# A linear-attention and PReLU network kernel: the first four steps in a new order, and GpSimd's fills ahead of its masks

## The chip, the cores and the metric

The kernel runs on one core of a Trainium2 chip. A core has five engines with queues of their own: TensorE (PE in the profile, its weight loads PEld), VectorE (DVE), ScalarE (ACT), GpSimd (POOL) and SyncE (SP, which here only issues DMAs). The metric is the time of one execution on the device in microseconds (us), as the median of several runs.

## The reference

Two blocks, one behind the other. For each of 4 batches and 8 heads, with 768 tokens of 48 dimensions, a gated linear attention:

```python
f = 1.0 / (1.0 + np.exp(-f_logit))
for t in range(S):
    state = f[:, :, t, :, None] * state + np.einsum('bhd,bhe->bhde', k[:, :, t], v[:, :, t])
    y[:, :, t] = np.einsum('bhd,bhde->bhe', q[:, :, t], state)
```

Its output, laid out as 3072 tokens of 384, goes through a network with 2048 hidden units:

```python
h = x @ w_in
g = np.maximum(h, 0.0) + alpha * np.minimum(h, 0.0)
return g @ w_out
```

All of it in float32.

## The kernel before

The work is cut into 12 **steps**: a step is one pair of batches (`bp`, 0 or 1) and one chunk `c` of 128 tokens (0 to 5), so steps 0 and 1 are the first chunk of both pairs, steps 2 and 3 the second, and so on. Within a chunk the recurrence is written as products: f is multiplied up over ranges of 4, 32 and 64 tokens, scores of q and k are formed within those ranges, masked into a matrix `A`, and `A` and the carried state multiply v.

Each stage of a step is a Python generator; every `yield` ends a piece. The order in which all pieces are emitted is written out by hand in the string `START` (up to step 4; `USUAL` repeats a pattern from step 5 on). That order is the queue order of TensorE, VectorE, ScalarE and SyncE. Each of these takes its instructions strictly in it and waits at the first one whose inputs or buffers aren't ready. GpSimd's order is not written out: a planner makes it from the order in which the instructions are emitted and from what it takes to be ready.

The letters of the string, with the number of the step behind them; P1.3 below means the third piece of P in step 1:

- **P** prepares. P.1 loads f, q, k, v (on SP for step 0, on GpSimd's queue for steps 1 to 4). P.2 on ScalarE: sigmoid of f (L298), copies of f and q (L299, L301). P.3 on VectorE: products of f (`kr`, `fs`) and q times f (`qd`; L310 to L320). In the first chunk (steps 0 and 1): P.4 has ScalarE's copies into the tile `us` (L341, L343), k times its products (L354), L355 and the first small products (L378, L383, L385); P.5 has L387, which writes `k16` inside `us`, L390 and L378; P.6 two scans (L347, L348) and the keys `kh`, `ks` (L414, L419); P.7 the queries `q3` (L408, L447); P.8 ScalarE's copies of them into `A` (L454).
- **S** and **T** are the scores of the two halves u = 0 and 1 of a step: .1 TensorE k times `qd` (L580, PSUM `pair0` or `pair1`), .2 VectorE's masked copies into `ad` (L589), .3 TensorE k4 times `us` (L580), .4 masked copies again (L615 in the first chunk, L599 later).
- **O** carries the state. In the first chunk: .1 TensorE `k16` times `q16` (L490), .2 ScalarE's copies into `ad` (L495), .3 VectorE L503 and TensorE `kh` times `q3` (L512), .4 ScalarE's copies into `A` (L519), .5 eight transposes of `ks` on TensorE (L529), .6 ScalarE's copies to `ksn` (L533), .7 TensorE `ksn` times v (L543), .8 ScalarE's copies into the state (L559). Step 0 uses the PSUM tiles `more0` and `more1`, the others `pair0` and `pair1`.
- **Y** attends: .1 and .2 ScalarE's copies of `ad` into `A` (L623), .3 TensorE `A` times v (L634), .4 ScalarE's copy y (L641), VectorE's update of the state (L553, twice L557) and, for all steps but the first, ten DMAs that turn y into xT (L664). Step 0 turns it on TensorE in Y0.5 instead (xt, L653, copied by L655).
- **n** is the network: eight pieces of ph (L679: twelve matmuls of 128x256), ScalarE's neg (L684) and VectorE's gate (L686), then the product with w_out (po, L699, for step 0; pa to pe, L718, later).
- **a** and **w** bring w_in in eight pieces of 256 columns: a issues the load on SP into one of three buffers (L234) and has ScalarE take it apart (L238, L239), w has VectorE put it together (L248). **b** and **g** do the same for w_out. The first load writes into a buffer that P0.2 touches last, so that it goes out behind q. In step 0, the k-th ph needs the k-th piece of w_in. **W** (L784) forms sums of w_out's quarters.
- **X** gives the PSUM tiles `more0` and `more1` back; the network's four banks and xt's come out of them.
- **i** multiplies ones by ones (L790, 128x256) and **j** does 16 tiny matmuls (L798). Both write `more0`, and nothing reads it.
- **K**, **M** (from step 2 on) move the keys by DMA.

The constants are filled and the masks are made on GpSimd before the first step: `mraw` (for L589), `mquad` (for L599), `mhalf` (for L615), `ident` and `dense` (for Y0.5), and two fills inside `us` for each of steps 0 and 1, `k16[16:32]` to zero (L335) and `g16[3:5]` to one (L336), which stand in P.4.

Of the kernel before, what the change touches and what calls it, by code (L numbers as in the profile page):

```python
# [8 lines left out]
F32 = mybir.dt.float32  # L9
I16 = mybir.dt.int16  # L10
# [8 lines left out]
DB = 32  # L19
MASKED = (1, 0)  # L20

U = 2
CH = 64
NC2 = C // CH
NB = DB // 4
WP = 768
RAWS, LEADS = 3, 4
# [1 line left out]

BEGUN = 5  # L30
START = (
    "i P0:4 j T0 P0:2 S0 P0 a O0:2 T0 P1 P0 O0 T0 S0 O0 P1 S0 a O0 P1 T0 S0 P1 O0:2 Y0 i P1 Y0 O0 S1 w Y0 "
    "a Y0 X a w O1 Y0 w O1 w S1 P1 a n0 w a:2 P1 n0 a T1 P1 P2 b S1 T1 S1 n0 w:2 n0 T1 O1 P2 T1 b P2 n0 w "
    "O1 g n0 b O1 P2 g:2 b Y1 g b P2 n0:2 O1 n0 O1 b:3 g:2 O1 g n0 Y1:2 g W:2 P2 n0 Y1 T2 W S2 P2 P3 T2 "
    "S2 P3 n0 n1 P3 T2 S2:2 T2 n1:3 P2 K2 Y2 W O2 T3 n1 Y2 T3 n1 M2 W O2 n1:2 O2 P3 n1 P3 O2 P3 n1 Y2:2 "
    "n1 P3 n1 S3 K3 n1 S3 n2 T3:2 P4 S3 n2:2 S3 n2 P4 n2:2 M3 P4 n2:3 P3 O3:3 Y3 O3 P4 Y3 n2 P4 Y3 n2 Y3 "
    "P4 S4 T4 S4 n2 T4 P5 n2 P4 n3:2 K4 P5 n3 S4 T4:2 n3 S4 n3:2 M4 P4 P5 n3:2 Y4 O4:2 Y4 O4 n3 P5 n3 O4 "
    "Y4:2 P5 n3:2 P5:3 K5 n3 "
)
USUAL = "T:2 S:2 n:4 M T:2 S n P+ S n P+ n:3 Y O P+ O:2 Y O n P+ Y:2 P+ n:3 P+:3 K+"  # L40

LOOSE = ("a", "w", "b", "g", "W", "i", "j", "X")

def flat(start, usual, steps=12):
    out = []
    for word in start.split():
        key, _, times = word.partition(":")
        out += [(key,) if key in LOOSE else (key[0], int(key[1:]))] * int(times or 1)
    for n in range(BEGUN, steps + 1):
# [11 lines left out]
def kernel(  # L61
# [30 lines left out]
    nc = tc.nc  # L92
    B, NC, _, HP, _ = qT.shape
    DM = v.shape[-1]
    H = 2 * HP
# [5 lines left out]
    W = U * HP * C  # L101
    GC = W // CH
    G = W // DB
    NJ = C // DB
    NQ = 4
    UO = [0, 0]
    for m in range(1, NB):
        UO.append(UO[-1] + (DB if m == 1 else DB - 4 * m))
    UW = UO.pop()
    VO = [0, 0, DB, DB + 16]  # L110
    VW = DB + 24
# [6 lines left out]
    work = ctx.enter_context(tc.tile_pool(name="work", bufs=2))  # L118
    staging = ExitStack()
    stage = staging.enter_context(tc.tile_pool(name="stage", bufs=1))  # L120
# [41 lines left out]

    mraw = const.tile([128, 4, NB, 4], F32, tag="mraw", name="mraw")
    nc.gpsimd.memset(mraw, 0.0)
    diag = lvl[:, 1].rearrange("p (i r) -> p i r", r=4)
    for d in range(4):
        nc.gpsimd.tensor_copy(mraw[:, d, :, d:4], diag[:, :, 0:4 - d])
    inq = const.tile([128, NB], F32, tag="inq", name="inq")
    nc.vector.tensor_reduce(inq, diag, mybir.AxisListType.X, ALU.add)
    mquad = const.tile([128, UW], F32, tag="mquad", name="mquad")  # L170
    nc.gpsimd.memset(mquad, 0.0)
    for m in range(1, NB):
        lo = UO[m] + (4 if m == 1 else 0)
        n = NB - m
        nc.gpsimd.tensor_copy(mquad[:, lo:lo + 4 * n].rearrange("p (i r) -> p i r", r=4),
                              inq[:, 0:n].unsqueeze(2).broadcast_to((128, n, 4)))
    mhalf = const.tile([128, VW], F32, tag="mhalf", name="mhalf")
    nc.gpsimd.memset(mhalf, 0.0)
    for half in range(2):
        for m in range(1, NQ):  # L180
            n = NQ - m
            lo = 16 * half + 4 if m == 1 else VO[m] + 4 * n * half
# [4 lines left out]


    A = const.tile([128, U, H, C], F32, tag="A", name="A")
    nc.gpsimd.memset(A, 0.0)  # L190
    ident = const.tile([128, 128], F32, tag="ident", name="ident")
    make_identity(nc, ident)
    nc.gpsimd.tensor_scalar(om, om, -1.0, 1.0, ALU.mult, ALU.add)
# [3 lines left out]
    nc.gpsimd.memset(dense, 0.0)  # L197
    for par in range(2):
        nc.gpsimd.tensor_copy(dense[:, (2 + par) * D:(3 + par) * D], ident[:, 64 * par:64 * par + D])

    first = {"raw": stage.tile([128, WP, 4], I16, tag="raw", name="w_in_raw0", bufs=RAWS)}

    def load_weights(dst, src, name):

# [60 lines left out]
    def quads(t):  # L265
        return t.rearrange("p (n r) -> p n r", r=4)

    def halves(cc):

        return slice(CH * cc, CH * cc + CH), slice(CH * (1 - cc), CH * (1 - cc) + D)  # L270

    def prepare(bp, c, x):

        i = f"{bp}_{c}"
        b0 = U * bp
        ahead = steps.index((bp, c))
        loads = nc.gpsimd if 0 < ahead < 5 else nc.sync

        def load(name, src, bufs=2):
            t = work.tile([128, W], F32, tag=name, name=f"{name}_{i}", bufs=bufs)  # L280
            tu = t.rearrange("p (u x) -> p u x", u=U)
            parts = [slice(u, u + 1) for u in range(U)] if name == "f" and not ahead else [slice(0, U)]
            for p in parts:
                loads.dma_start(out=tu[:, p], in_=src[b0:b0 + U, c].rearrange("u p h t -> p u (h t)")[:, p])
            return t

        f = quads(load("f", fT, 1))
# [3 lines left out]
        for cc in range(NC2):  # L291
            t_, _ = halves(cc)
            loads.dma_start(out=vs[bp][t_, cc, :, 0:DM], in_=v[b0:b0 + U, c, t_].rearrange("u t d -> t u d"))
        yield

        by_u = [slice(u * G * NB // U, (u + 1) * G * NB // U) for u in range(U)] if not ahead else [slice(0, G * NB)]
# [28 lines left out]


        ps = work.tile([128, NS], F32, tag="ps", name=f"ps_{i}", bufs=1)
        ut = work.tile([128, G * UW], F32, tag="us", name=f"us_{i}", bufs=1)
        if c:
            us = ut.rearrange("p (g t) -> p g t", g=G)  # L330
        else:

            at = (0, VW, VW + 16, VW + 16 + DB, VW + 16 + DB + NB)
            us, q16, k16, g16 = (ut[:, G * lo:G * hi].rearrange("p (g t) -> p g t", g=G) for lo, hi in zip(at, at[1:]))
            nc.gpsimd.memset(k16[:, :, 16:DB], 0.0)  # L335
            nc.gpsimd.memset(g16[:, :, 3:5], 1.0)  # L336
            x["q16"], x["k16"] = q16, k16
        x["us"] = us
        q4 = us[:, :, 0:DB].rearrange("p g (i r) -> p g i r", r=4)
# [136 lines left out]
    def carry(bp, c, x):  # L476

        i = f"{bp}_{c}"
        home = more if (bp, c) == steps[0] else pairs
        off = home[0]  # L480
        if not c:
            half = home[1]
            for u in range(U):
                for hp in range(HP):
                    for j in range(NJ):
                        g = (u * HP + hp) * NJ + j
# [8 lines left out]
                nc.scalar.copy(ad[:, u, :, :, 16:DB], half[:, :, o:o + HP * 16].rearrange("p r (h t) -> p r h t", h=HP))  # L495
            yield
        q3, ks, kh, pre = (x[n] for n in ("q3", "ks", "kh", "pre"))
        f64 = work.tile([128, U, H], F32, tag="f64", name=f"f64_{i}")
        by64 = pre.rearrange("p (a c j) i -> p a c j i", c=NC2, j=2)
        for cc in range(0 if c else 1, NC2 if c < NC - 1 else 1):  # L500
            for par in range(2):
# [3 lines left out]
        for u in range(U):  # L505
            for hp in range(HP):
                a = (u * HP + hp) * NC2
# [15 lines left out]
        if not c:  # L523
            yield
            pk = home[1]
            for u in range(U):
                for hp in range(HP):
                    a = (u * HP + hp) * NC2
# [281 lines left out]
    with tc.manual_schedule(engines={mybir.EngineType.PE, mybir.EngineType.DVE, mybir.EngineType.Activation,  # L810
                                     mybir.EngineType.SP}):
        run = {}
        for n, step in enumerate(steps):
            x = {}
            for key, stage_ in zip("POYKMn", (prepare, carry, attend, keys_moved, landed, network)):
                run[key, n] = stage_(*step, x)
            run["S", n], run["T", n] = (scores(u, *step, x) for u in range(U))
        for key in ORDER:
            next(run[key] if key in run else pieces[key[0]])
# [55 lines left out]
```

## Time and profile before

| | before |
|---|---|
| median of 3 runs | 602.92 us (602.43 to 603.97) |
| profiled execution | 602.81 us, span 601.0 us |
| busy: TensorE, VectorE, ScalarE, GpSimd | 575.6, 494.7, 247.4, 85.4 us |
| mean granted clock of TensorE | 0.999 |
| DMA | 50.36 MB |

The span is the time from the first to the last instruction; 1.8 us of the execution lie around it. A row of the profile names the source line, engine, operation and tiles, the number of instructions, and what ended the engine's idle time before them; the chain of waits follows the work that ended last back from the end. On TensorE a float32 matmul of the program stands as two matmuls. A few records of matmuls can be missing.

### The profile page before, as it was taken

The page shows a single profiled execution, that of the slowest core. Times are in us where ns is not written, and L with a number is a line of the kernel's source. Part 1 is how long each engine was busy: PE and PEld are TensorE (multiplying, and loading weights), DVE is VectorE, ACT ScalarE, POOL GpSimd, SP SyncE. Part 2 cuts the span into 40 slices and gives each one's busy share as a digit, 9 for nine tenths or more (in the row PEclk, how much of TensorE's full clock was granted, in tenths as well). Part 3 has the DMA queues.
Part 4 walks back from the last instruction along what each step waited for, and adds up shares of the span by engine and source line. Part 5 has one row for each costly group of instructions (what it writes and reads, how often), then busy time and mean ns, then how long its engine had stood idle before and what let it go on. Part 6 is the DMA issues. An engine that isn't in the chain of part 4 may idle for free.

```text
span 601.0 us, 18092 instructions
## 1 busy us (share of the span) xinstructions
PE 575.6 (96%) x7760; PEld 516.8 (86%) x7760; DVE 494.7 (82%) x998; ACT 247.4 (41%) x430; POOL 85.4 (14%) x162
## 2 busy tenths in 40 slices
PE   2489999999999999999999999999999999999997
PEld 1378667898899899899899899899899899899997
DVE  7989998997888779988988988988988987882351
ACT  5679952621461450550461451452343344232110
POOL 9210014013002103001200300300300300300000
PEclk9999999999999999999999999999999999999999
DMA  8778736015005302502601601601601511201000
GB/s 263 254 216 295 249 89 125 1 48 130 2 2 161 52 1 59 156 1 56 157 2 55 159 3 56 158 2 41 170 4 30 155 31 27 55 1 29 27 1 27
DMA packets 52880, 50.36 MB, mean 84 GB/s; under 512 B 26720, under 2 KB 43360, under 8 KB 52800
## 3 DMA queue, kind: packets, MB, share of 16 engines
q1 hardware_dynamic: 42784, 37.46, 21.7%
q0 software_dynamic: 5504, 9.90, 6.7%
q10 hardware_dynamic: 4512, 1.85, 1.3%
q8 instruction: 61, 1.00, 0.7%
q14 instruction: 19, 0.16, 0.1%
HBM read 36.21 MB, written 4.72 MB: 68 GB/s over the span
## 4 chain that ended last, share of the span: by engine, by line
PE 88%; DVE 7%; ACT 2%; POOL 1%; issue 1%; DMA 0%; DVEq 0%; ACTq 0%; POOLq 0%
PE ph L679 40%; PE pa L718 10%; PE pc L718 10%; PE pair L580 6%; PE pe L718 5%; PE pd L718 5%; PE pb L718 5%; PE pair L634 3%; PE pair L543 1%; DVE w_out_sb L248 1%; PE pair L512 1%; PE po L699 1%; DVE gate L686 1%; POOL mhalf L183 1%; DMA f<-in_fT 0%
## 5 line engine op out<-in xcount | busy, mean ns | idle before, releaser
L679 PE MATMUL ph<-xT,w_in_sb 128*128 128x256 f32 x1152 | 255.3, 381 | 1.4 <-DVE w_in_sb L248 1.4
L679 PEld LDWEIGHTS ph<-xT,w_in_sb 128*128 128x128 f32 x1152 | 216.9, 190 | 33.4 <-issue 2.4
L686 DVE SCALAR_TENSOR_TENSOR gate<-neg,om,ph 128x256 f32<-128x256 f32 x192 | 81.2, 476 | 33.0 <-ACT neg L684 33.0
L684 ACT ACTIVATE neg<-ph 128x512 f32<-128x512 f32 x96 | 56.1, 594 | 121.2 <-PE ph L679 101.6
L718 PE MATMUL pa<-w_out_sb,gate 128*128 128x192 f32 x352 | 62.1, 330 | 0.0
L718 PE MATMUL pc<-t,S 128*128 128x192 f32 x352 | 61.6, 328 | 0.0
L454 ACT COPY A<-q 48x512 f32<-48x512 f32 x44 | 27.1, 617 | 83.4 <-DVE q L408 82.9
L718 PEld LDWEIGHTS pa<-w_out_sb,gate 128*128 128x128 f32 x352 | 57.4, 190 | 1.3
L464 POOL DMA_DIRECT2D ksn<-kt x80 | 46.2, 586 | 85.9 <-DVE kt L422 61.3
L718 PEld LDWEIGHTS pc<-t,S 128*128 128x128 f32 x352 | 57.4, 190 | 0.4
L664 POOL DMA_DIRECT2D xT<-y x22 | 11.9, 544 | 287.5 <-ACT y L641 287.4
L599 DVE COPY_PREDICATED ad<-mquad,pair 128x224 f32<-128x224 int32 (+6 forms) x140 | 41.7, 299 | 4.1
L589 DVE COPY_PREDICATED ad<-mraw,pair 128x256 f32<-128x256 int32 (+1 forms) x96 | 41.2, 451 | 4.0 <-PE pair L580 0.8
L364 DVE TENSOR_TENSOR us<-us,fs 128x768 f32<-128x768 f32 (+5 forms) x60 | 36.9, 615 | 1.1
L765 DVE TENSOR_TENSOR S<-gate 128x512 f32<-128x512 f32 x44 | 30.3, 688 | 0.8
L718 PE MATMUL pe<-w_out_sb,S 128*128 128x192 f32 x176 | 30.6, 327 | 0.0
L718 PE MATMUL pb<-t,gate 128*128 128x192 f32 x176 | 30.4, 326 | 0.0
L718 PE MATMUL pd<-w_out_sb,S 128*128 128x192 f32 x176 | 30.4, 326 | 0.0
L623 ACT COPY A<-ad 32x512 f32<-32x512 f32 x48 | 29.4, 613 | 0.6
L641 ACT COPY y<-pair 128x512 f32<-128x512 f32 x22 | 11.8, 589 | 43.4 <-PE pair L634 43.4
L718 PEld LDWEIGHTS pe<-w_out_sb,S 128*128 128x128 f32 x176 | 28.8, 190 | 0.2
L718 PEld LDWEIGHTS pb<-t,gate 128*128 128x128 f32 x176 | 28.9, 190 | 0.0
(125 smaller groups left out, 710.6 us busy)
## 6 DMA issues: line engine op xcount, KB each, us to landing
w_out_raw<-in_w_out SPq DMA_DIRECT2D x8, 767.8 KB, 7.9
w_in_raw<-in_w_in SPq DMA_DIRECT2D x8, 767.2 KB, 9.5
out<-o SPq DMA_DIRECT2D x23, 192.0 KB, 1.9
q<-in_qT SPq DMA_DIRECT2D x8, 512.0 KB, 4.6
k<-in_kT SPq DMA_DIRECT2D x8, 512.0 KB, 7.1
f<-in_fT SPq DMA_DIRECT2D x7, 512.0 KB, 3.9
vs<-in_v SPq DMA_DIRECT2D x16, 192.0 KB
ksn<-kt SPq DMA_DIRECT2D x80, 32.0 KB, 2.2
```

What stands on the lines that cost most here:

```text
L364: nc.vector.tensor_tensor(us[:, :, UO[m]:UO[m] + 4 * n].rearrange("p g (i r) -> p g i r", r=4), us[:, :, skip:skip + 4 * n].rearrange("p g ...
L454: nc.scalar.copy(A[halves(cc)[1], :, par * HP:(par + 1) * HP, CH * cc:CH * (cc + 1)], q3[rows(par)].rearrange("p (u h c) s t -> p u h c (s ...
L464: (nc.gpsimd if a % 2 else nc.sync).dma_start(out=ksn[32 * b:32 * (b + 1)].rearrange("p u (h x) -> p (u h) x", h=HP)[:, :, 32 * a:32 * a + n],
L580: nc.tensor.matmul(to[DB * j:DB * (j + 1), par, hp * step + lo:hp * step + hi], lhsT=keys[r_, g * DB:(g + 1) * DB], rhs=by[r_, g, lo:hi], ...
L589: nc.vector.copy_predicated(adu[:, :, :, d:4], mraw[:, d, :, d:4].bitcast(I32).unsqueeze(1).broadcast_to((128, H, NB, n)), rv[:, :, QO[d]: ...
L599: nc.vector.copy_predicated(ad[:, u, :, :, 4 * m:DB], mquad[:, lo:lo + n].bitcast(I32).unsqueeze(1).unsqueeze(1).broadcast_to((128, 2, HP, ...
L623: nc.scalar.copy(A[s_].rearrange("p u h t -> p (u h) t")[:, :, s_], ad[s_].rearrange("p u r h t -> p (u r h) t"))
L679: nc.tensor.matmul(ph[:, j * T:(j + 1) * T], lhsT=w_in_sb[:, kt, m * 128:(m + 1) * 128], rhs=xT[:, kt], start=(kt == 0 and j == 0), stop=( ...
L684: nc.scalar.activation(neg, phv, AF.Relu, scale=-1.0)
L686: nc.vector.scalar_tensor_tensor(gate[:, m % NH, m // NH], neg[:, j], om[:, m:m + 1], phv[:, j], ALU.mult, ALU.add)
L718: nc.tensor.matmul(to[:, 0:DH], lhsT=of(f), rhs=by(f), start=(f == 0 and not more), stop=(f == NH - 1), skip_group_check=True)
L765: nc.vector.tensor_tensor(to, x_, y_, op)
```

## The change

Three things change.

- `START` is a new order of the same pieces. Both `i` are gone, the one `j` moves behind S0.4, and from the pieces around step 5 on the order is as it was. In the new order step 0's P0.5 follows P0.4 directly; S goes ahead of T in step 0; step 1's P1.2 stands ahead of O0.4; the first piece a1 stands behind O0.4 and P1.3 in place of ahead of O0.1; P1.4 and P1.5 stand together ahead of Y0.1, O0.5, S1.1 and O0.6; O1.1 stands behind Y0.5 in place of ahead of it; w7 and w8 stand behind n0.4; Y1.3 stands behind n0.11.
- Step 0's fills of `us` (L335, L336) are emitted directly behind `mraw`'s fill and ahead of all masks, by a function `of_halves`. The fill of `A` moves behind `dense`.
- `mquad` is filled in a function that is called behind step 1's loads (P1.1).

`f64` is also kept in the step's dictionary, and `LOOSE` has one more letter; neither adds an instruction.

```diff
 START = (
-    "i P0:4 j T0 P0:2 S0 P0 a O0:2 T0 P1 P0 O0 T0 S0 O0 P1 S0 a O0 P1 T0 S0 P1 O0:2 Y0 i P1 Y0 O0 S1 w Y0 "
-    "a Y0 X a w O1 Y0 w O1 w S1 P1 a n0 w a:2 P1 n0 a T1 P1 P2 b S1 T1 S1 n0 w:2 n0 T1 O1 P2 T1 b P2 n0 w "
-    "O1 g n0 b O1 P2 g:2 b Y1 g b P2 n0:2 O1 n0 O1 b:3 g:2 O1 g n0 Y1:2 g W:2 P2 n0 Y1 T2 W S2 P2 P3 T2 "
...
+    "P0:3 S0 P0:2 T0 O0 P0:2 O0 P1 S0 O0 P1 S0 O0 T0 S0 j P1 a T0 P0 T0 P1:2 w Y0 O0 S1 O0 Y0 O0:2 a Y0:2 "
+    "a P1 w P1 X Y0 w O1 a w a:2 n0 O1 S1 w a n0 w a n0:2 w:2 b O1 T1:2 O1 n0 b g n0 g b S1 T1:2 b P2 n0 "
+    "P2 S1 b P2 g n0 g P1 n0 O1 b O1 b g:2 Y1 n0 O1 g b Y1 O1 S2 P2 n0 g S2 P2 W P2 Y1:2 P2 n0 T2 O2 P3 "
...
     nc.gpsimd.memset(mraw, 0.0)
+    at = (0, VW, VW + 16, VW + 16 + DB, VW + 16 + DB + NB)
+
+    def of_halves(ut):
+
+        parts = [ut[:, G * lo:G * hi].rearrange("p (g t) -> p g t", g=G) for lo, hi in zip(at, at[1:])]
+        nc.gpsimd.memset(parts[2][:, :, 16:DB], 0.0)
+        nc.gpsimd.memset(parts[3][:, :, 3:5], 1.0)
+        return parts
+
+    first = {"us": work.tile([128, G * UW], F32, tag="us", name="us_first", bufs=1)}
+    first["parts"] = of_halves(first["us"])
...
     mquad = const.tile([128, UW], F32, tag="mquad", name="mquad")
-    nc.gpsimd.memset(mquad, 0.0)
-    for m in range(1, NB):
-        lo = UO[m] + (4 if m == 1 else 0)
...
-    nc.gpsimd.memset(A, 0.0)
...
+    nc.gpsimd.memset(A, 0.0)
...
+    def quads_of_mask():
+
+        nc.gpsimd.memset(mquad, 0.0)
+        for m in range(1, NB):
...
+        if ahead == 1:
+            quads_of_mask()
         yield
...
-            nc.gpsimd.memset(k16[:, :, 16:DB], 0.0)
-            nc.gpsimd.memset(g16[:, :, 3:5], 1.0)
+            us, q16, k16, g16 = of_halves(ut) if ahead else first["parts"]
```

## The prediction

> **What bounds the kernel now.** Read first: busy shares by slice (15 us each), on the page.
>
> ```profile
> PE   2489999999999999999999999999999999999997
> DVE  7989998997888779988988988988988987882351
> ```
>
> From the third slice on TensorE is full, to the end. Its matmuls are the same before and after (bar two warming pairs), so the span is the time at which the full stretch begins, plus that work, plus holes in it. The second view, what TensorE waited for, gives the holes:
>
> ```profile
> PE pair L580 <- ACT us L341: 5.7, 1, 5.7
> PE more L543 <- ACT ksn L533: 3.5, 1, 3.5
> PE more L490 <- DVE us L390: 3.4, 1, 3.4
> PE more L512 <- DVE q L408: 2.3, 1, 2.3
> PE ph L679 <- DVE w_in_sb L248: 1.4, 1, 1.4
> PE more L490 <- issue: 0.6, 1, 0.6
> ```
>
> All but the 1.4 fall before 40 us (the timeline puts that one at 64.92 to 66.28; after 42.55 there is only one more, 0.25 at 87.87). Third, the chain of waits in order of time, which tells who is late in the first 40 us:
>
> ```profile
> 6.27 2.35 POOL mquad L175 x5
> 8.62 3.44 POOL mhalf L183 x6
> ...
> 13.46 0.22 POOL us L336
> ...
> 13.70 0.69 DVE us L387
> ...
> 23.18 1.07 ACT f L298
> ...
> 29.65 1.08 ACT ksn L533 x2
> ...
> 32.31 1.15 PE more L790 x2
> 33.46 1.27 PE pair L580 x64
> 34.73 2.81 PE more L634 x60
> ...
> 39.89 2.83 PE xt L653 x12
> ```
>
> GpSimd's masks hold VectorE, VectorE and ScalarE hold TensorE; 32.31 is the second warming pair `i`. Last, TensorE's timeline, for its pace:
>
> ```profile
> 25.36 1.97 PE L529 MATMUL more<-ident,ks 128*128 128x128 f32 x8
> 37.56 1.58 PE L490 MATMUL pair<-us 48*32 48x16 f32 x128
> 61.29 1.04 PE L529 MATMUL pair<-ident,ks 128*128 128x128 f32 x8
> ```
>
> The same eight transposes take 1.97 us at 25 and 1.04 at 61: 214 and 109 ns apart. TensorE begins at half pace. In step 0's L634 the timeline has 34 matmuls from 34.66 to 36.53 (55 ns each) and 30 from there to 37.56 (34 ns); the trace's record of the granted clock sets in at 36.65 (the page's PEclk, full from the start, tells nothing of the time ahead of it). The full clock came 5.87 us into the one long unbroken run of the start, which begins at 30.78 with L543. Nothing shorter brought it (25.36 to 27.33, for one).
>
> **The change part by part.** Pieces are named by step and place: P1.3 is the third piece of P of step 1.
>
> *GpSimd's fills.* VectorE waited 1.49 us at L387 (12.21 to 13.70) for the fill L336. That fill now precedes the masks, so the wait goes whole. Moving mquad's seven copies (3.05 us) behind step 1's loads lets those issue sooner: GpSimd reached them at 13.55, so 10.5 now, but f's old contents are read until 11.4 (L355), so about 11.5. mquad itself is first read at 102.74 (L599): 90 us of cover, cost nothing. If that cover were gone, 3.05.
>
> *VectorE.* From L387 at 12.21: P0.5 to P0.7 take 6.65 (13.70 to 20.35), giving 18.86; S0.2 1.60, the two L503 0.49, T0.2 1.60: 22.55; S0.4 (half of L615's 1.82) 23.46; P1.3 3.64: 27.10; T0.4 0.91: 28.0. Before, both halves were done at 29.73, so 1.7 earlier: the 1.49 and 0.2 that P1.3 waited for the sigmoid. No wait of VectorE's lies in between if step 1's f is ready by 23.5.
>
> *ScalarE.* The first weight piece a1 (L238, L239: 1.6) moves from 12.2 to behind O0.4, P1.2 moves ahead of O0.4. From P1.2 to the end of P1.4 it has 2.7 + 1.5 + 1.6 + 1.25 (L454) + 2.4 = 9.4 us of work and must be through by 28.0, so P1.2 must start by 18.6. f lands 3.9 us (its row's median) to 5.4 (k's) after an issue at 11.5, at 15.4 to 16.9, so it holds. Behind P1.2 wait O0.4, then `j` on TensorE (it writes the PSUM that O0.4 reads), then T0.3; T0.3's result isn't wanted before 27.1, so 3 us of slack.
> Then Y0.1 1.25 (28.05 to 29.3), O0.6 1.08 (30.4), L543 1.53 (32.0), L559 0.96 (33.0), and L634 starts at 33.1 where it started at 34.66. The removed second `i` (1.15) lay on that path, but L543 could not start before L533, so its removal is within these 1.5 us and not added again. The first `i` lay in a 5.66 us wait for others: nothing.
>
> *L634 to the network.* At half pace throughout, 64 x 55 ns = 3.5: to 36.6 (before 37.56). To xt it was 2.35 (L553, both L557): xt at 38.95, against 39.89. But O1.1 (L490, 1.41 busy) ran in that wait before and now stands behind xt: 38.95 + 2.66 (39.89 to 42.55) + 1.41 = 43.0 for the first ph, against 42.55. At an equal clock +0.5.
>
> *The clock.* Before, an unbroken run from 30.78 to 38.4 (L543, `i`, S1.1, L634, O1.1) brought it ahead of xt. Without `i`, with S1.1 moved ahead of O0.6 and O1.1 behind xt, the run is broken at 32.0 (1.1 us, for L559) and at 36.6 (2.35). The longest stretch before xt is L634 itself, 3.5. From xt on nothing breaks it, so by the 5.87 us of before the grant comes at 44.8. Until then xt costs 12 x 427 = 5.1 in place of 2.66 (twice 213.5 ns for twice the columns; +2.5) and half of O1.1 at 1.6 in place of 1.4 (+0.1): +2.6. From below: nothing, if L634 brings the clock; from above: +5, if O1.1's small matmuls don't count and the 5.87 start behind them. I take 2.6, the nearest row's.
> The Trainium skill, "TensorE: Matmul & The Clock Gate", Part 1, says that the array runs at half clock until one whole window of about 3.4 us has been busy, that windows run free of the kernel, and that idle gaps should be avoided: this speaks against the change. The two L529 rows agree with the factor. By it the grant would come 3.4 to 6.8 us after xt begins, an estimated loss of 1.7 to 2.8.
>
> *Weight pieces.* The fourth w_in load waits on SP for a1's buffer: issued at 13.92, now about 23. Behind it on SP stand only weight pieces until 83.71. w2 to w8 come later, but in the new order each stands one or two pieces ahead of the ph that reads it, and ph begins 3 us later. The 1.36 wait at 64.92 (n0.8 behind w8) should go, since w8 moves from behind S1.4, T1.4 and P2.3 (6 us of VectorE) to behind n0.4; and the 0.25 at 87.87 (T2.1 behind y's L557), since n0.12 now lies between. That is -1.6; from above 0, if VectorE (4.9 of 5 us busy from 60 to 85) is as late by another item.
>
> *TensorE's fetches.* Waits marked issue are 0.6 at 15.93 and 0.4 at 22.94. With the fourth weight load gone from 14 to 20 us they may go, but VectorE sets the pace there (TensorE has 2 to 3 us of slack), so 0; without that cover, 1.0.
>
> *Later steps.* Y1.3 moves behind n0.11: between its end and the first ph of step 1 stand po (5.4), T2.1 (0.8) and L512 (0.65), 6.9 in all. From L634's end to the last landing of xT took 5.5 (82.5 to 88.0: y, four issues of 0.7 on ScalarE's queue, 2 to land), so 1.4 of slack: nothing.
>
> Sum: 0.5 + 2.6 - 1.6 = +1.5. The profiled execution took 602.81 (span 601.0 and 1.8 around it), 0.1 under the median of 602.92. Forecast 602.81 + 1.5 = 604.3.
>
> **The rivals.**
> *The clock comes in L634* (ends faster). It decides if a run of 3.5 us or less is enough. Then L634 takes 2.8 as before (-0.7), the 2.6 is not paid, xt starts at 38.2 and ph at 42.3: -0.2, and with -1.6 the time is 601.0. For it: only one run in the profile was ever long enough to tell, so 5.87 is an upper bound. Against: the 4 us from 23.35 to 27.33, with one hole of 0.23, brought nothing.
> *Step 1's loads come late.* GpSimd's order is made by a planner. If q and both pieces of v (0.9 MB) go ahead of f and all share with the weight pieces, they and f (1.44 MB) at half of the 323 GB/s of the stretch from 10 to 15 us take 8.9 us from 12.4 (issue at 10.5, first packets 2 us later, as the trace has them): f at 21.3, 2.7 behind the 18.6 that ScalarE needs. It moves L634 and xt by that much: 607.0. Against it: f, q, k, v was the order before.
> *The change does nothing of what it says* is excluded for the fills (L387 waits for L336 by name); for the fetches it is my reading that it pays nothing, and it is in the sum.
>
> **How the numbers follow.** A measurement of this kernel tells about 0.3% (1.8 us) from no change: the bounds are 601.1 and 604.7. Clock at half pace into xt: 0.62. Its centre lies just inside the bound, and its open costs (the clock up to +2.4 more, the 1.6 not won) lie above it more than below: 0.36 slower, 0.26 the same. Clock in L634: 0.25, at 601.0, 0.22 faster, 0.03 the same. Late loads: 0.13, 0.11 slower, 0.02 the same. Together 0.22, 0.31, 0.47. The range goes from 600.8, just under the fast rival, to 607.0, the late loads and the clock's upper bound in part. Of the likeliest case alone: 603.4 to 606.7.
>
> **What would show it.** Right: L387 starts at about 12.2 without a wait; L634 of step 0 at about 33 with 64 matmuls 55 ns apart to its end; xt taking about 5 us; ph's 216 ns pace only from about 44; no wait of TensorE's for w_in at L679. Wrong: xt's matmuls 216 ns apart (then 601), a wait of ScalarE's for f beyond 18.6 (then later), or new waits of TensorE's after 46.

## The result, and the profile after

| | before | after |
|---|---|---|
| median (lowest to highest, 20 runs each) | 602.54 us (601.54 to 606.72) | 605.30 us (602.06 to 607.49) |
| ratio of after to before, 95% interval | | 1.0035 [1.002, 1.005] |
| profiled execution, span | 602.81, 601.0 | 603.97, 602.2 |

The new order is slower, by 0.2 to 0.5%: the ratio makes 2.1 us, the two medians differ by 2.8. Single executions of either kernel spread over some 5 us, so times below are medians of several runs with an interval, while a profile, being one run, only shows what happens in it. The profile after was taken in a run 1.3 below its kernel's median. The line numbers used below are 13 to 16 higher after the change (L580 is now L593, L634 L647, L653 L666, L679 L692, L589 L602, L615 L628, L387 L400, L298 L314).

Busy shares by slice, on the page of the kernel after:

```profile
PE   1469999999999999999999999999999999999997
DVE  8888899999878889788987988988988987882351
```

TensorE's first and third slices are emptier (1 and 6 for 2 and 8), VectorE's first is fuller (8 for 7). What TensorE waited for, in the same run (six of ten rows):

```profile
PE more L503 <- issue: 2.2, 1, 2.2
PE xt L666 <- DVE vs L570: 2.2, 1, 2.2
PE more L556 <- ACT ksn L546: 1.9, 1, 1.9
PE pair L593 <- issue: 1.8, 1, 1.8
PE pair L593 <- ACT f L314: 1.7, 1, 1.7
PE more L647 <- ACT vs L572: 0.7, 1, 0.7
```

The 1.4 for w_in at 64.92 and the 0.25 at 87.87 are gone. Longer are two waits marked "issue", 2.2 and 1.8 (before 0.6 and 0.4); new by name is one for step 1's sigmoid `f`; the wait ahead of xt is 2.2 (before 0.75). The chain of waits of the same run between 12 and 46 us:

```profile
12.62 8.16 DMA f<-in_fT
...
20.86 1.07 ACT f L314
...
23.00 1.84 issue
...
25.33 0.42 DVE ad L628
...
33.40 1.58 PE more L556 x64
...
36.02 3.28 PE more L647 x56
...
41.64 2.83 PE xt L666 x12
44.47 1.19 PE pair L503 x80
```

GpSimd's fills no longer hold VectorE: L400 starts at 13.10 without a wait (before at 13.70, behind 1.49 of waiting). In its place the chain names the load of step 1's f (landed at 20.78) and, behind that, 1.84 us in which TensorE waits for none of the engines and VectorE waits for TensorE (1.40 at L628). The first of these is a near tie. VectorE's timeline after, and then in e3 (an experiment below):

```profile
19.76 2.06 DVE L602 COPY_PREDICATED ad<-mraw,pair 128x256 f32<-128x256 int32 x4
25.33 1.16 DVE L628 COPY_PREDICATED ad<-mhalf,pair 128x224 f32<-128x224 int32 x3 [1.40 <-PE pair L593]
```

```profile
19.02 2.08 DVE L602 COPY_PREDICATED ad<-mraw,pair 128x256 f32<-128x256 int32 x4
```

After, the L593 at 21.97 starts 2.21 behind the start of these copies (S0.2), and 0.04 behind the sigmoid's end. In e3 it starts at 21.24, 2.22 behind them, and there the profile names the copies as what it waited for. In e1, e2, e6, e7, e8 and e9 the distance is 2.20 to 2.22 too, though the sigmoid starts anywhere from 16.01 to 20.12. So that matmul would have started at 21.97 with an earlier f as well, and what is new on the path is the 1.84. The first ph stands at 45.59, against 42.55. From the first ph to the last matmul it is 553.31, against 555.23.

**What "issue" is here.** Queue q8 on the page carries instructions: 61 packets, 1.00 MB, so 16 KB each. TensorE executes 7756 matmuls and as many weight loads, which makes one packet for 128 pairs. In the trace the two stops end at matmuls 223 and 351 in both kernels, 128 apart, and the packet for a block begins some us after the block before it is entered. Before: block entered at 10.20 (128 weight loads ahead of the first stop's end), next packet begins at 14.16, its first instruction runs at 16.55; then 16.55, 20.63, 23.35. After: 11.40, 15.38, 17.84; then 17.84, 22.09, 24.84. So while the loads of step 1 and of w_in move, a block of 128 pairs took 6.4 to 7.0 us in these two runs. Before, that pace cost next to nothing. After, it starts 1.2 later: 0.65 of it because the first scores start that much later (9.99 against 9.34; q of step 0 landed later in this run), the rest because `i` and the early `j` (34 pairs) no longer use up a part of the first block while TensorE waits for its inputs. The third block, whose results VectorE now wants earlier, comes 1.5 later.

The stops are not of the new order's making. The four other profiles with the old order (e4, e10, e11 and e12 below) have them at 2.0 to 2.5 and 1.2 to 2.1, as long as after the change, and in none of them does VectorE wait at L615 (L628 in e4): in the old order P1.3 lies ahead of these copies, in the new one behind them. What the new order took away is the cover.

### The profile page after: what moved, and what is told of

It is laid out like the page before. It is cut to its first block, busy times and chain, and to the rows that moved or that the text cites. A ratio compares the mean times of both kernels' runs of the same rounds, so it can differ in the third digit from the quotient of the medians.

```text
span 602.2 us, 18075 instructions
## 1 busy us (share of the span) xinstructions
PE 573.3 (95%) x7756; PEld 515.9 (86%) x7756; DVE 495.1 (82%) x998; ACT 247.5 (41%) x430; POOL 83.7 (14%) x162
## 4 chain that ended last, share of the span: by engine, by line
PE 90%; DVE 4%; DMA 1%; POOL 1%; issue 1%; ACT 1%; ACTq 1%; DVEq 0%; POOLq 0%
PE ph L692 42%; PE pa L731 9%; PE pc L731 9%; PE pair L593 6%; PE pb L731 5%; PE pe L731 4%; PE pd L731 4%; PE po L712 3%; PE pair L647 3%; PE pair L556 1%; DMA f<-in_fT 1%; PE pair L525 1%; ACTq L677 1%; DVE vs L570 1%; PE more L647 1%
## 5 line engine op out<-in xcount | busy, mean ns | idle before, releaser
L692 PE MATMUL ph<-xT,w_in_sb 128*128 128x256 f32 x1152 | 255.2, 381 | 0.1
L692 PEld LDWEIGHTS ph<-xT,w_in_sb 128*128 128x128 f32 x1152 | 216.9, 190 | 31.9 <-ACT neg L697 0.9
L731 PE MATMUL pc<-t,S 128*128 128x192 f32 x352 | 61.6, 328 | 0.0
L602 DVE COPY_PREDICATED ad<-mraw,pair 128x256 f32<-128x256 int32 (+1 forms) x96 | 41.4, 450 | 3.1 <-PE pair L593 0.3
L593 PE MATMUL pair<-qd,k 48*32 48x80 f32 x1536 | 21.1, 248 | 11.9 <-DVE qd L326 11.9
L593 PEld LDWEIGHTS pair<-qd,k 48*32 48x32 f32 x1536 | 18.1, 111 | 14.8 <-ACT us_first L354 10.0
L731 PE MATMUL pe<-w_out_sb,S 128*128 128x192 f32 x176 | 30.5, 327 | 0.2 <-ACT o L752 0.2
L735 DVE SCALAR_TENSOR_TENSOR Csum<-pc,Csum 128x192 f32<-128x192 f32 x22 | 7.8, 354 | 27.8 <-PE pc L731 27.5
```

The costliest lines, as they stand in the source:

```text
L593: nc.tensor.matmul(to[DB * j:DB * (j + 1), par, hp * step + lo:hp * step + hi], lhsT=keys[r_, g * DB:(g + 1) * DB], rhs=by[r_, g, lo:hi], ...
L602: nc.vector.copy_predicated(adu[:, :, :, d:4], mraw[:, d, :, d:4].bitcast(I32).unsqueeze(1).broadcast_to((128, H, NB, n)), rv[:, :, QO[d]: ...
L692: nc.tensor.matmul(ph[:, j * T:(j + 1) * T], lhsT=w_in_sb[:, kt, m * 128:(m + 1) * 128], rhs=xT[:, kt], start=(kt == 0 and j == 0), stop=( ...
L731: nc.tensor.matmul(to[:, 0:DH], lhsT=of(f), rhs=by(f), start=(f == 0 and not more), stop=(f == NH - 1), skip_group_check=True)
```

## The experiments

All have 10 or 12 runs, beside 33 to 35 of the kernel before on the same chip. e1 to e4 share a chip (before there 602.34), then e5 to e8 (602.71), then e9 to e12 (602.62). e5 and e10 to e12 have the line numbers of before.

| | median, lowest to highest | ratio to before, 95% |
|---|---|---|
| e4_fills_only | 602.80 (601.16 to 607.40) | 1.0010 [0.9994, 1.0026] |
| e5_order_only | 605.16 (603.93 to 607.50) | 1.0034 [1.0017, 1.0052] |
| e1_head | 604.78 (602.47 to 607.63) | 1.0043 [1.0026, 1.0059] |
| e2_gaps | 604.09 (601.55 to 605.93) | 1.0021 [1.0003, 1.0040] |
| e3_o1 | 604.13 (602.61 to 606.83) | 1.0031 [1.0015, 1.0046] |
| e6_all | 604.11 (602.40 to 607.51) | 1.0026 [1.0004, 1.0049] |
| e7_weights_late | 604.63 (601.63 to 605.98) | 1.0018 [0.9999, 1.0037] |
| e8_all_late | 604.12 (603.38 to 607.21) | 1.0023 [1.0004, 1.0043] |
| e9_filled | 604.01 (601.21 to 606.04) | 1.0018 [0.9999, 1.0037] |
| e10_w8 | 603.42 (601.68 to 604.72) | 1.0005 [0.9986, 1.0024] |
| e11_w8_no_i | 602.83 (601.32 to 604.22) | 1.0000 [0.9977, 1.0022] |
| e12_o1_behind | 603.42 (601.76 to 606.43) | 1.0014 [0.9996, 1.0032] |

My theory was that the order costs the clock ahead of xt and moves O1.1 onto the path; the rivals were late loads and instruction fetches.

**Which of the two parts?** e4_fills_only has the old `START` with the new order of GpSimd's fills; e5_order_only has the new `START` with the old one.

> The order of before with the new order on GpSimd alone (us filled ahead of the masks, mquad behind step 1's loads). VectorE's 1.49 us wait at L387 goes. Order and clock stay as before, so by my sum's first term VectorE and then ScalarE's chain run 1.5 earlier up to L533, L543, L634 and xt: 1.0 to 1.5 below before, 601.0 to 601.5. Rival: ScalarE's chain takes it back (P1.2 there stands behind O0.4, f of step 1 lands late): same as before, 602.5.

> The new order with GpSimd as before (us filled behind the masks, mquad ahead of step 1's loads). Clock theory: the breaks around L634 are there, so the loss against before is that of the whole change or more: 604.5 to 606. Fetch theory (a block of 128 matmuls of TensorE's program takes about 6.4 us to fetch while weights are loading, whatever VectorE does, so that VectorE's 1.5 us are worth nothing): the same as the whole change, 605.3, since the fills bring nothing. My sum without the fetches: 1.5 worse than the whole change, 606.8.

The order alone costs as much as the whole change (605.16, against 606.8 by the sum without the fetches), the fills alone can't be told from no change. Why fills which take a 1.49 wait off the chain gain less than that is seen in e4's chain of waits:

```profile
2.13 7.42 DMA k<-in_kT
...
9.64 1.23 DVE k L367
...
12.80 0.69 DVE us_first L400
```

With GpSimd out of the way, step 0's k, landing at 9.55, sets when VectorE gets to L400: 12.80, 0.9 earlier than before, not 1.49. In that profile the first ph is 0.91 earlier than before and the last matmul 0.53; twelve runs don't show it. Nor is the 1.49 always there to be won. It stands in the profiles of before and e12, where GpSimd's `mhalf` took 3.50 and 3.49; with the same order on GpSimd it took 2.47, 1.56 and 1.24 in e5, e10 and e11, and there L387 starts at 13.11, 13.54 and 12.91 without a wait.

In e5 the stop for instructions is at the same place as in the kernel after (VectorE's timeline):

```profile
25.59 1.02 DVE L615 COPY_PREDICATED ad<-mhalf,pair 128x224 f32<-128x224 int32 x3 [1.85 <-PE pair L580]
```

**The warming pairs and O1.1, one at a time.** e1 puts the pairs back at the head, e2 in the gaps ahead of xt, e3 puts O1.1 back ahead of Y0.5; all three are edits of the kernel after.

```diff
 e1: - "P0:3 S0 ... T0 S0 j P1 a        + "i P0:3 j S0 ... T0 S0 P1 a
 e2: - w Y0 O0 S1 O0 Y0 O0:2 a Y0:2     + w Y0 O0 i S1 i:2 O0 Y0 O0 j O0 a Y0:2
 e3: - "a P1 w P1 X Y0 w O1 a w         + "a O1 P1 w P1 X Y0 w a w
```

> The changed kernel with i ahead of P0 and j ahead of S0.1, where TensorE waits anyway, and no j later: TensorE has 36 more instruction pairs behind it when O0.1 begins, as before the change. Fetch theory (TensorE's instruction fetches now fall due inside O0.1 and S0.3, and the 1.84 us at 23.0 holds VectorE for 1.40 at L628): the fetches fall due at the end of S0.1 and inside S0.3's wait again, the two issue waits shrink from 2.2 and 1.8 to about 0.6 and 0.4, xt starts about 1.4 earlier, the median is 1 to 1.5 below the changed kernel's 605.3: about 604. Clock theory (TensorE's full clock comes at a moment that depends on a window that runs free of the kernel, in most runs only behind xt): median unchanged within 0.5, the spread of runs as wide as the changed kernel's 5 us. Late-loads theory (step 1's f, 8.2 us in coming, sets the pace): unchanged.

> The changed kernel with matmuls that nothing reads in TensorE's waits between the transposes and L634 of step 0: one i behind O0.5, two behind S1.1, j behind O0.7. Clock theory: the stretch from the transposes to the end of L634 is nearly unbroken (10 us), the full clock comes ahead of xt in every run, the median falls by about 2 to some 603, and the runs spread by about 2 us in place of 5. Fetch theory: unchanged, 605 (the matmuls stand behind the two waits). Late-loads theory: unchanged. The i's overrun their wait by up to 0.4 us at half pace, which is in the 603.

> The changed kernel with O1.1 ahead of Y0.5, as before the change, so that it fills 1.2 of the 2.2 us that TensorE waits ahead of xt. My sum (0.5 for the ph that begins 1.4 later because O1.1 stands in front of it): 1.2 less, about 604.1 in the median. Clock theory adds: the hole ahead of xt shrinks from 2.2 to 0.9, so the clock comes sooner in some runs; 603.5 to 604. Fetch and late-loads theories alone: only the 1.2.

None returns to the kernel before. e1 is as slow as the kernel after. e2 and e3 stand 1.2 lower by medians, with intervals that still hold the whole loss (so that e3 met its 604.1 says little). But e2's windows show what the hole ahead of xt does (columns: stretch, its length, busy time with instructions in brackets of TensorE, its weight loads, VectorE, ScalarE and GpSimd, then TensorE's granted clock, the DMA share and GB/s):

```profile
37.20:40.60 3.40, 1.15 (x25) 0.99 (x22) 2.85 (x5) 3.06 (x5) 1.21 (x2) 1.00 0.43 110
40.70:44.00 3.30, 3.30 (x10) 2.59 (x9) 3.27 (x6) 0.74 (x2) 0.00 (x0) 0.50 1.04 313
44.10:47.40 3.30, 3.30 (x139) 2.76 (x138) 3.18 (x6) 2.77 (x5) 0.00 (x0) 1.00 0.46 167
```

The extra pairs had brought the full clock at 33.8. A stretch with 1.15 of 3.40 us busy, the 2.25 hole in it, was followed by one at half clock, 3.41 long in the record, and xt fell into it: 4.51 for its twelve matmuls in place of 2.83. Of e2's 12 runs 11 have a mean clock of 0.997 or less (one lost stretch is half of 3.41 in some 570 us, 0.003) and a median of 604.2; the one at 1.000 took 601.55.

**All three, and the loads.** e6 has the edits of e1, e2 and e3 together. In e7 (else the kernel after) and e8 (else e6) the first weight loads wait for step 1's sigmoid in place of step 0's q:

```diff
-        if not ahead:
-            nc.scalar.copy(first["raw"]..., q[:, 0:1])
+        if ahead == 1:
+            nc.scalar.copy(first["raw"]..., f[:, 0, 0:1])
```

> The changed kernel with all three: i and j at the head, matmuls in the waits up to L634, O1.1 ahead of xt. Clock theory: TensorE is unbroken for over 10 us and the hole ahead of xt is under 1 us, so the clock comes ahead of xt and isn't taken back; the late waits stay away: 601.5 to 602.5, and no wider a spread than before's. Fetch theory alone: 604.8 as with the head alone. Late-loads theory alone: 604.

> The changed kernel with the first three weight loads held back until step 1's sigmoid (about 20 us in place of 8): between 9 and 20 us only step 1's own loads move. Fetch theory: the second block's packet comes about 1.2 us after its turn in place of 4, the issue waits of 2.2 and 1.8 nearly vanish, L628 doesn't wait, L634 starts 1.5 to 2 earlier; median 603 to 604. Late-loads theory: f lands 4 us after its issue in place of 8.2, ScalarE doesn't wait for it. If weights are then late for a1 (about 25), ScalarE waits up to 1 us. If fetches are slow for another reason than the weights, the two issue waits stay near 2.

> All four edits: i and j at the head, matmuls in the waits, O1.1 ahead of xt, and the first weights held back. If fetch and clock theories both hold, their gains add: 1.5 to 2 below the run without the late weights: 600 to 601, below before. If the fetches don't matter once the clock is there: as without, 602.

e6 stays above what the clock theory gave and near the 604 of the late-loads theory alone, e7 is above what the fetch theory gave, and e8 above both of its values. ScalarE's timeline after, and then in e7, at step 1's sigmoid:

```profile
20.86 1.06 ACT L314 ACTIVATE f<-f 128x1024 f32<-128x1024 f32 x1 [1.95 <-DMA f<-in_fT]
```

```profile
16.01 1.06 ACT L314 ACTIVATE f<-f 128x1024 f32<-128x1024 f32 x1 [0.39 <-DMA f<-in_fT]
```

With the weights held back f takes 4.21 to land, not 8.16; the packet for the second block begins 0.86 after the first is entered (10.65 to 11.51), not 3.98; VectorE's wait at L628 is gone; and VectorE sees the end of L647 (L566) at 37.12, not 39.39. So the late loads and the late instructions go together: both shrink when the weights are held back. Of the 2.3 at L566, 1.40 is the wait at L628. The other 0.9 VectorE already has at L602 (18.88 against 19.76), and e1, e3 and e9 have it too (18.97 to 19.06) with the weights at their old place, so it belongs to the run. The median falls by 0.7. e7's timeline shows what took it back there: the hole ahead of xt is still 2.25, the clock had come early enough (36.62) to be lost by it, and xt took 4.51.

```profile
39.38 4.51 PE L666 MATMUL xt<-y,dense 128*128 128x256 f32 x12 [2.25 <-DVE vs L570]
```

In e6 that hole is 0.5 and the first ph stands at 42.19, 3.4 earlier than after. The end is only 0.8 earlier (last matmul 598.11 against 598.91), because TensorE now runs into VectorE's backlog (e6's timeline; the third pieces of S and T of step 1):

```profile
59.96 0.82 PE L593 MATMUL pair<-us,k 48*32 48x52 f32 x64 [0.40 <-ACT A L532]
62.21 0.82 PE L593 MATMUL pair<-us,k 48*32 48x52 f32 x64 [1.42 <-DVE ad L602]
```

Nor did the clock stay, as was expected of e6: granted at 27.61, it was taken back from 34.43 to 37.85, over L647, and 10 of its 12 runs have a mean clock of 0.997 or less (9 of 12 in e8).

**The hole filled.** e9 is e1 and e2 plus three matmuls of ones, which nothing reads, in the wait ahead of xt.

> The kernel after, with the warming pairs of the kernel before put back at the head and in the gaps, and three matmuls of ones (nothing reads them) in the 2.2 us in which TensorE waits ahead of step 0's transposes xt; O1.1 stays behind xt. Theory 'the clock is taken by the hole ahead of xt': the record shows one grant before 41 us, not withdrawn ahead of the first ph; xt takes 2.5 us, the first ph stands at 43.5 to 44.5, the median is 602.5 to 603.5 (0.5 to 1.5 below the variant with the pairs in the gaps, 604.09). Rival 'the order itself is later, the clock has no part in it': no change against that variant, 604.0 or more (the three matmuls may overrun the wait by up to 1.2).

```profile
36.56 1.56 PE L809 MATMUL pair<-ones 128*128 128x256 f32 x6
38.89 2.83 PE L666 MATMUL xt<-y,dense 128*128 128x256 f32 x12 [0.76 <-DVE vs L570]
41.64 1.26 PE L503 MATMUL pair<-us 48*32 48x16 f32 x128
42.84 3.50 PE L692 MATMUL ph<-xT,w_in_sb 128*128 128x256 f32 x15
```

In the profiled run xt went as the clock theory said: no loss there, ph at 42.84, and 601.21, the lowest of all runs of this table but one. The median is 604.01 all the same, within 0.1 of e2, so the theory's number failed. The single grant that was expected isn't there either: the clock came at 26.38 and was gone from 29.79 to 33.20, ahead of L647's main part, and 9 of the 12 runs have a mean clock of 0.997 or less. What the other runs of e9 lose is not explained by the hole ahead of xt.

**Single terms, on the kernel before.** e10 moves w8 ahead of P2.3, e11 also takes the second `i` out, e12 moves O1.1 behind Y0.5.

```diff
 e10: - n0 T1 O1 P2 T1 b P2 n0 w        + n0 T1 O1 P2 T1 b w P2 n0
 e11: e10, and  - Y0 i P1 Y0 O0 S1 w    + Y0 P1 Y0 O0 S1 w
 e12: - X a w O1 Y0 w O1 w S1           + X a w Y0 w O1:2 w S1
```

> The kernel before, with one piece moved: w8 stands ahead of P2.3 and not behind n0.8's place. It tests the term -1.6 of the prediction by itself. If w8 stands where VectorE is late only because of P2.3, TensorE's 1.36 wait for w_in at 64.92 goes, and the median falls by 1.1 to 1.4, to 601.2 to 601.5; this would beat both kernels. Rival 'VectorE is full from 60 to 85, another item is as late': the wait comes back under another name within 10 us, and the median stays at 602.3 to 602.8.

> The variant with w8 ahead of P2.3, and without the second warming pair (32.31 to 33.46). If that pair has no part in the clock, the time is the same as with it, or up to 0.5 less (VectorE and ScalarE set L634's start). Rival 'it fills the window that brings the clock ahead of L634': the grant comes one window of 3.4 us later, which costs 1.7 in a good part of the runs: the median rises by 0.5 to 1.5 and the runs spread more.

> The kernel before, with O1.1 moved from ahead of Y0.5 to behind it, one move of the change by itself. The prediction's sum for that alone: the 1.41 of O1.1 no longer lies in TensorE's wait ahead of xt but on the path, less nothing: the first ph at 43.9 (42.55 + 1.4) and the median at 603.9. Theory 'the hole of 2.2 ahead of xt also costs the clock for a window': 1.7 more in many runs, median 604.5 to 605.5, and in a disturbed run the record shows the clock withdrawn for 3.4 us about xt. Rival 'O1.1 finds other cover': median within 0.4 of the kernel before.

e10: the wait for w_in at 64.92 goes, nothing is gained. What TensorE waited for in e10, the entries after 59 us (its profiled run, 604.72, is the slowest of the twelve):

```profile
PE pair L580 <- DVE vs L557: 0.8, 1, 0.8
PE ph L679 <- DVE w_in_sb L248: 0.5, 1, 0.5
PE pair L634 <- ACT A L623: 0.4, 1, 0.4
```

That is 1.7 in place of 1.6: VectorE is late by the next item, as the rival had it. e11: the second pair is worth nothing that 12 runs can tell. e12's windows:

```profile
36.40:39.70 3.30, 1.13 (x38) 0.99 (x34) 2.09 (x4) 2.07 (x4) 1.21 (x2) 1.00 0.63 213
39.80:43.10 3.30, 3.30 (x8) 2.67 (x9) 2.74 (x3) 0.85 (x2) 0.00 (x0) 0.50 0.87 222
```

The one move opens the hole (2.25), and the clock goes for one stretch, in the order of the kernel before, with the fills and loads untouched. The median, 603.42, falls between the expectations, and the runs fall in two groups: 6 of the 12 have a mean clock of 0.997, with a median of 604.6; the others 602.7, near the kernel before's 602.62. Of the 103 runs of before in the three comparisons 18 stand below 0.999. So in e12 the hole costs a clock stretch in half the runs, some 2 us each, about 1 on average. In other variants a lost stretch doesn't sort the runs like that (in e1 the four runs with one have a median of 604.5, the six without 605.15).

O1.1's own 1.4, which the sum put on the path, costs nothing at full clock that can be seen: in the profiled run the first ph is 2.86 later than before, and the stretch from there to the last matmul is 1.23 shorter. From the start of xt to the last matmul it is 559.63 against 557.89 before, and xt alone took 1.67 longer at half clock; without that it would be 557.96.

## Why the prediction was right, and where it was not

The total was right: 604.3 forecast, 605.3 measured, inside 600.8 to 607.0, and on the slower side, which had the largest chance. The first ph came at 45.59; 43.0 and the 2.6 for the clock make 45.6 in the sum. That is luck: in the profiled run xt started at 41.64, 2.7 later than the sum's 38.95, and the 2.6 for the clock wasn't paid. Several terms were wrong and made up for one another.

- *The fills.* Right that L387's wait goes whole (L400 has none), and that moving `mquad` showed no cost. "At about 12.2" holds in six profiles with the new fills (e1, e3, e6 to e9: 12.19 to 12.39), not in after (13.10), e2 (12.76) and e4 (12.80): step 0's loads are the next in line, and they land later in some runs (after, q by 0.6; in e4 it is k). And the 1.49 isn't in every run: in e5, e10 and e11 VectorE doesn't wait there, though GpSimd has its old order.
- *VectorE 1.7 earlier at T0.4.* Failed. "No wait of VectorE's lies in between" was the wrong step: S0.4 waited 1.40 for TensorE, and T0.4's copies ended at 31.0, not 28.0. L634 started at 34.87 with its main part at 36.02, not at 33.1.
- *TensorE's fetches, 0 ("without that cover, 1.0").* This is the term behind it. The cover of 2 to 3 us of slack was gone: in all seven profiles with the new order and the weights at their old place VectorE waits at that point, by 0.74 (e6) to 2.25 (e3), and with the weights late it doesn't (e7, e8). Taking out the first `i` and `j` made it worse: without them the wait is 1.40 to 2.25 (after, e2, e3, e5), with them 0.74 to 1.01 (e1, e6, e9).
- *ScalarE and the loads.* "f at 15.4 to 16.9, so it holds" failed: it landed at 20.78, 2.2 beyond the 18.6. That was the second rival's mechanism, near its 21.3, though the order f, q, k, v was kept and no planner had put f last; the traffic with the weights was enough. The term was sized by the wrong row: f's 3.9 is a median over the whole execution, while in the first 30 us of before the loads on GpSimd's queue had k at 10.3 and v at 10.0. The rival's 2.7 wasn't paid, because f's lateness and the stop for instructions lie side by side: with the stop, VectorE's T0.4 ends at 30.98, and ScalarE, late by f, is through its copies at 30.87. Without the stop f would have held ScalarE to some 30.5 (an estimate: 30.87 less the 0.40 that its last copy waited for VectorE), so each alone would have cost something.
- *The clock, 2.6.* The likeliest case had xt at half pace; in the profiled run xt ran at the full pace (2.83), granted at 40.09, after one stretch of 3.41 us of which L634 filled all but 0.6. So 5.87 unbroken us are not needed, as the first rival said. Nor did the prediction's "nothing shorter brought it" (the 4 us from 23.35 to 27.33) hold up: e10 and e11 have the same pieces in the same order there, and the clock came right behind them, at 28.52 and 26.82. TensorE was busy for 3.15 of the 3.41 us from 25.11 in e10 and for 3.39 of the 3.41 from 23.41 in e11; before, counted back from its grant, the stretch from 23.00 had 2.83. By these three it matters where the stretches fall, and that differs from run to run. (The unbroken run of before also lasted longer than the 38.4 that the prediction read, to 39.14.) And "wrong: xt's matmuls 216 ns apart (then 601)" is what the profile shows; it wasn't 601, because L634 was 1.8 late (34.87 against 33.1) and the hole ahead of xt 2.2 long. What I had not priced was the other direction: a clock that had come can be taken back by the hole in front of xt (e2, e5, e7, e12; xt took 4.50 or 4.51 in each). The Trainium skill, "TensorE: Matmul & The Clock Gate", Part 1, has free windows of 3413 ns, and every stretch in the records here is 3.41 or a multiple, but for the last, which the record cuts off. The Trainium skill speaks there of an idle window before the clock is taken. Here a stretch with 1.13 of 3.30 us busy was enough, and in e3 (at 61.6, far behind xt) one with 1.82 of 3.30. The measurement decides: a window about half idle, or a third busy, can be enough. It need not be: after itself kept the clock with 1.55 of 3.41 idle (40.09 to 41.64), and e1 with 1.86 of 3.41 (38.70 to 42.11). What those two had in the busy part is xt, e3 small matmuls; whether that makes the difference no run here tests.
- *The late waits, −1.6.* The waits went, and the stretch behind the first ph became 1.92 shorter. But the cause was not where I put it. Moving w8 alone (e10) gives nothing back, and starting ph later alone (e12) gives 1.23. The reading that fits both is that VectorE's backlog from 59 to 90 us sets when TensorE can go on, so a late ph is partly forgiven and an early ph (e6) partly taken back. The "from above 0, if VectorE is as late by another item" was the right value for the edit.
- *O1.1 behind xt, +1.4.* Over-priced for the same reason (e12's runs without a lost stretch: 602.7).

**What stays open.** The loss belongs to the order (e4, e5). The uncovered stop for instructions and the hole ahead of xt are both shown in profiles: without the one (e7, e8) VectorE's wait goes, without the other (e9) xt keeps its clock. Their shares of the 2 us are not settled: each remedy takes back 0.5 to 1.3 of the difference in medians, all of them together (e8, 604.12) no more than one, and the intervals overlap. A clock taken back can't be the main part in the kernel after itself: 15 of its 20 runs have a mean clock of 1.000, and their median is 605.34. A first grant that comes late isn't seen in that mean, since the record starts with it, so the forecast case (xt at half pace) may well be what most of these runs had; only a trace of such a run near the median could tell. The nearest trace is that of e5 (605.54, the order alone). There xt began 1.60 later than before and ran at half pace, with O1.1 behind it, so that the first ph was 4.57 later, and 1.89 of this came back by the last matmul: 2.7, the difference in medians. But its half pace is a clock taken back (granted at 38.63, gone from 42.04 to 45.45), not one that hadn't come. No variant beat the kernel before.

## What to carry to other kernels

Before a wait is priced as gained, find the next arrival on the same engine, the loads and TensorE's instruction packets included, and look in several profiles whether the wait is there each time. A wait that an order covers, as P1.3 did here, belongs in the sum of any order that takes the cover away. Ahead of a stretch that runs full behind a second engine's backlog, a start that is 3 us earlier may be worth less than 1, so test each term of a sum by one edit on the kernel before. And look at how full the last clock window is in front of large matmuls: a hole of 2.2 us there cost another 1.7 in four profiles (e2, e5, e7, e12), and nothing in two (after, e1).

## What the hardware showed that I had not expected

- TensorE's program arrives in packets of 16 KB, one per 128 pairs of weight load and matmul; the packet for the second block began 0.9 us after the first was entered where the weights weren't loading (e7, e8) and 3.7 to 5.3 us after it where they were (the other twelve profiles); its first instruction ran 2.3 to 2.5 us after the packet began in those twelve.
- The granted clock changes only in steps of 3.41 us. A stretch with L634 in all but 0.6 us of it granted the full clock; stretches with 1.13, 1.15 and 1.82 of 3.3 to 3.4 us busy were followed by one at half clock, one with 1.55 of 3.41 (e1) was not.
- GpSimd's six small copies for `mhalf` took 1.24 to 3.50 us in five profiles with the same order on GpSimd (before, e5, e10, e11, e12), and 1.21 after, where they stand 4 us earlier; no run here separates why.
